# The first loads of an attention kernel: wq on ScalarE's queue, K and V in whole transfers from the first pack on

## The chip, the cores and the metric

The kernel runs on one core of one Trainium2 chip. The metric is the device time of one execution in microseconds (us). Before the change it is 732.18 us, the median of three runs (731.67 to 732.88). A profile of one execution was taken beside them. All times "at" some us are counted from the start of the profiled span.

## The reference

Two independent attention blocks, A and B, have the same shapes; their outputs stand side by side. For each block:

```python
B, Sq, D = 16, 64, 640          # x
H, Sk, Dh = 32, 512, 128        # k_cache, v_cache: [B, H, Sk, Dh]
q = (x @ wq).reshape(B, Sq, H, Dh).transpose(0, 2, 1, 3)      # wq: [640, 4096]
scores = einsum("bhqd,bhkd->bhqk", q, k_cache) * Dh ** -0.5
p = softmax(scores, axis=-1)
o = einsum("bhqk,bhkd->bhqd", p, v_cache)
out = o.transpose(0, 2, 1, 3).reshape(B, Sq, H * Dh) @ wo     # wo: [4096, 640]
```

Everything is bfloat16. K and V are read once each, 64 MiB per cache and block, so most of what the kernel moves is K and V.

## The kernel before, in words

**Packs, groups, phases.** A pack `n` is two batches by four heads: 1 MB (2 x 512 KB) of K and 1 MB of V. There are 128 packs. Four packs (`NJ`) form a group: the same two batches, 16 heads. Eight groups (`NBP`) form a phase of 32 packs: all batches with one half of a block's heads. Four phases (`ph`) cover A's two halves and then B's. A phase has its own half of wq (five transfers of 512 KB, `LDWQ`, one for each 128 rows of wq, in rows of 4 KB) and its own half of wo (four blocks of 640 KB, `LDWO`, in rows of 1280 bytes).

**The steps of a pack.** `XT`/`XE`/`XS`/`XC` transpose the group's x tile and put it where the projection reads it (`xT_ring`). `WP` (GpSimd, L656) reorders wq from `ws_sb` into `wqp_sb`; two copies per pack index make one pack's part, and the first of them waits for all five transfers. `QP` (TensorE, L688) is the q projection, `QE` scales q. `KT` (VectorE, L702) transposes K. `S` (L712) is the scores, `EX` (ScalarE) the exponential with its row sum, `RC` (VectorE) the reciprocals, `NM` (GpSimd) the multiplication by them. `TR` (TensorE, L774) and `TE` (VectorE) transpose the probabilities, `PV` (L867) multiplies them by V, `OE` evicts, `OP` (L887) multiplies by wo and adds up in PSUM. PV and what follows for a pack run about two packs behind its scores: TensorE does QP(n), PV(n-2), S(n), TR(n-1), OP(n-2) in turn. So the pipeline begins with packs -2 and -1, which have zeros in place of data. TensorE's instructions form a loop of four packs.

**The order of work.** `build_plan` makes all operations with a nominal time in packs (`AT`); each engine's order follows these times, and the waits are worked out from what the operations read and write. SP's list of loads is ordered by times of its own: in the kernel before, the first phase's five `LDWQ` come first (-50), then K of packs 0, 1, 2, the second group's x, V of pack 0, the first wo block, K 3, V 1, wo, K 4, V 2, wo, K 5, V 3, and so on. SP issues in this order and waits, where it has to, for a place in a ring: K has six places, V four. In V's ring, the places 2 and 3 are held at the start by the zeros of packs -2 and -1, so V of pack 2 waits for `TR(-1)`, V of pack 3 for `TR(0)`, V of pack 4 for `TR(1)`.

**Queues.** SP's transfers run on the DMA queue that the page calls q1, ScalarE's on q10. In the kernel before, ScalarE issues only the first x tile (`LDX`, L608). Each K and V ring place and each part of wq has a semaphore of its own; a first load from ScalarE has one of its own, too (`d_first`).

**Transfers.** The constant `KSPLIT` = 8 makes the first eight packs' K come in four transfers of 256 KB (L629) and their V in two of 512 KB (L646; the second half has another semaphore, and `TE` waits for the first, `PV` for the second). Later packs have two transfers of 512 KB for K (L631) and one of 1 MB for V (L641). The last two packs (`NARROW`) have their V in two parts in any case. The rows are the same in both forms: 8 KB for K, 4 KB for V.

The lines that decide this:

```python
apart = 0 <= n < cfg.KSPLIT or n >= N - cfg.NARROW
...
if i < 2 or n < cfg.KSPLIT:
    op = add("sp", "LDK", (n, i), n + AT["KT"] - 0.9, [], [("kn", n % cfg.NK)])
    loads.append((n - cfg.NV + AT["PV"] + 0.2 - cfg.KLEAD, 2, op))
```

Of the kernel before, what the change touches and what calls it, by code (L numbers as in the profile page):

```python
# [20 lines left out]
class Cfg:  # L21
# [8 lines left out]
    PERIOD = 4  # L30
    BASE = 32
    KLEAD = 2.5
    KSPLIT = 8
    NARROW = 2
    AFTER = 24
    AT = dict(XT=-2.585, XE=-2.383, XS=-1.65, XC=-0.788, QP=-0.428, QE=-0.224, KT=-0.672, S=0,
# [50 lines left out]
def build_plan(dims, cfg, general):  # L87
# [4 lines left out]
    NPH, NBP, NJ = dims["NPH"], dims["NBP"], dims["NJ"]  # L92
    PH = NBP * NJ
    N = NPH * PH
    AT = cfg.AT
    ops = []
    loads = []
    at = {}

    def add(eng, kind, idx, ts, reads=(), writes=()):  # L100
        op = Op(eng, kind, idx, ts, reads, writes)
        ops.append(op)
        at[(kind, idx)] = op
        return op

    def add_output(n):
        g, j = n // NJ, n % NJ
        final = n >= 0 and dims["FINAL"](g // NBP)
        apart = 0 <= n < cfg.KSPLIT or n >= N - cfg.NARROW
        for b in range(0 if apart else 1, 2):  # L110
# [61 lines left out]
    for ph in range(NPH):  # L172
        twp = [ph * PH + t for t in AT["WP1" if ph else "WP0"]]
        for kt in range(dims["KT"]):
            ready = (twp[-1] - PH if ph > 1 else AT["WP0"][-1]) + 0.5
            op = add("sp", "LDWQ", (ph, kt), twp[0] - 0.5 if ph else -20.0, [], [("ws", kt, j) for j in range(NJ)])
            loads.append((ready + 2.0 + 0.14 * PH * kt if ph > 1 else AT["PV"] + 0.15 if ph else -50.0, 1, op))
        for j in range(NJ):
            w = ph * NJ + j
            n0 = ph * PH + j  # L180
            for i in range(2):
                add("pool", "WP", (w, i), twp[2 * j + i], [("ws", kt, j) for kt in range(dims["KT"])], [("wqp", j, i)])
            if ph:
                loads.append((n0 - NJ + AT["LDWO"], 4, add("sp", "LDWO", w, n0 + AT["OP"] - 0.8 * NJ, [], [("wo", j)])))
            else:
                loads.append((n0 - 1.9, 4, add("sp", "LDWO", w, n0 + AT["OP"] - 0.8 * NJ, [], [("wo", j)])))
# [6 lines left out]
    for n in range(-2, N):  # L193
# [3 lines left out]
        g, j = n // NJ, n % NJ  # L197
        add("pe", "QP", n, n + AT["QP"], [("xT", g % cfg.NX), ("wqp", j, 0), ("wqp", j, 1)], [("SB", 1)])
        add("act", "QE", n, n + AT["QE"], [], [("SB", 1), ("qs", n % cfg.NQ)])
        for i in range(4):  # L200
            if i < 2 or n < cfg.KSPLIT:
                op = add("sp", "LDK", (n, i), n + AT["KT"] - 0.9, [], [("kn", n % cfg.NK)])
# [65 lines left out]
    def for_pe(d):  # L268
        if d.kind == "EX":
            return d.idx % 4 == 1 or d.idx % 4 == 0 and d.idx // 4 % NJ == 1  # L270
        if d.kind == "OE":
            return d.idx[1] == 0
        if d.kind == "LDV":
            return d.idx[1] == 1
        if d.kind == "NM":
            return d.idx % 4 == 3 and d.eng == "pool"
        if d.kind == "OS" and d.idx == N // NJ - 1:
            return False
        return d.kind in own
# [44 lines left out]
    counts = dict(base)  # L324

    def sem_key(op):
        if op.kind == "LDX" and op.eng == "act":
            return ("d_first",) + op.writes[0]
        if op.kind == "LDV":
            return ("d_v" if op.idx[1] else "d_vh", op.writes[0][1])  # L330
        if op.kind in LOADS:
            return ("d_" + op.kind[2:].lower(),) + op.writes[0][1:]
        if op.kind in ("ST", "STH"):
            return ("d_out",)
        return ("q_" + op.eng,) if for_pe(op) else ("s_" + op.kind.lower() + "_" + op.eng,)

    for eng in ENGINES:
        for op in progs[eng]:
            op.sem = sem_key(op)
            counts[op.sem] = op.count = counts.get(op.sem, 0) + 1  # L340
# [164 lines left out]
def mha_kernel(nc, blocks, out, cfg=None):  # L505
# [16 lines left out]
    def wide(n):  # L522
        return n < NPACK - cfg.NARROW

    plans = []
    for general in (False, True):
        dims = dict(NPH=NPH, NBP=NBP, NJ=NJ, KT=KT, FIRST=lambda ph: ph % NSUB == 0,
                    FINAL=lambda ph: ph % NSUB == NSUB - 1)
        plans.append(build_plan(dims, cfg, general))
    NK, NV, NKT, NX, NXN, NQ, NPN, NRS = (cfg.NK, cfg.NV, cfg.NKT, cfg.NX, cfg.NXN, cfg.NQ, cfg.NPN, cfg.NRS)  # L530

    with contextlib.ExitStack() as es:
# [42 lines left out]
        def pack_info(n):  # L575
            g, j = n // NJ, n % NJ
            ph = g // NBP
            return ph // NSUB, g % NBP, j, ph % NSUB * HPH + 4 * j
# [45 lines left out]
        def em_LDK(e, op):  # L624
            n, b, l = op.idx[0], op.idx[1] // 2, op.idx[1] % 2
            blk, bp, j, h = pack_info(n)
            src = blocks[blk][1][2 * bp:2 * bp + 2, h:h + 4].rearrange("b h (p l t) d -> l (h p) b (t d)", l=2, t=32)[l]
            if n < cfg.KSPLIT:
                ins = e.dma_start(kn_ring[2 * b + l::4, n % NK].rearrange("p a c -> p (a c)"), src[:, b])  # L629
# [4 lines left out]
        def em_LDV(e, op):  # L634
# [3 lines left out]
            blk, bp, j, h = pack_info(n)  # L638
            if wide(n) and n >= cfg.KSPLIT:
                src = blocks[blk][2][2 * bp:2 * bp + 2, h:h + 4].rearrange("b h (p t) d -> (h p) b (t d)", t=16)  # L640
# [430 lines left out]
```

## Time and profile before

| | |
|---|---|
| median of three runs | 732.18 us |
| the profiled execution | 732.12 us, of which the span is 730.4 us |
| TensorE busy (matmul) | 674.1 us, 92% |
| VectorE, ScalarE, GpSimd busy | 514.5, 533.3, 417.9 us |
| moved by DMA | 295.02 MB, mean 404 GB/s |
| first slice of 18.26 us | 337 GB/s |
| first wq: issued by SP | 0.93 to 3.32 us |
| first q projection on TensorE | 15.48 us |
| first scores | 20.08 us |
| SP waits for TensorE's transposes before a V load (L641) | 251.1 us in 105 waits |

The busy shares are means over the whole span; the slices of the page and the stretches of the trace tell when. In lines of the timeline the columns are start, duration, engine, line, operation, tiles and count, and in brackets the idle time before it with what ended it. SPq and ACTq are the issues of DMAs on SP's and ScalarE's queue. In the table of stretches each engine has its busy time and in brackets the number of instructions; the last three columns are the granted TensorE clock, the DMA engines' mean busy share and the GB/s that they moved.

### The profile page before, as it was taken

The page shows a single profiled execution, that of the slowest core. Times are in us where ns is not written, and L with a number is a line of the kernel's source. Part 1 is how long each engine was busy: PE and PEld are TensorE (multiplying, and loading weights), DVE is VectorE, ACT ScalarE, POOL GpSimd, SP SyncE. Part 2 cuts the span into 40 slices and gives each one's busy share as a digit, 9 for nine tenths or more (in the row PEclk, how much of TensorE's full clock was granted, in tenths as well). Part 3 has the DMA queues.
Part 4 walks back from the last instruction along what each step waited for, and adds up shares of the span by engine and source line. Part 5 has one row for each costly group of instructions (what it writes and reads, how often), then busy time and mean ns, then how long its engine had stood idle before and what let it go on. Part 6 is the DMA issues. An engine that isn't in the chain of part 4 may idle for free.

```text
span 730.4 us, 61195 instructions
## 1 busy us (share of the span) xinstructions
PE 674.1 (92%) x28502; PEld 530.3 (73%) x28502; DVE 514.5 (70%) x691; ACT 533.3 (73%) x1574; POOL 417.9 (57%) x596
## 2 busy tenths in 40 slices
PE   1679999999999999999997899999999799999998
PEld 1458778787777777777775677787777577787775
DVE  5447777777777766767765667677777567878775
ACT  1447878778787777777875677777778677878775
POOL 4436565666875455554884555465587446555552
PEclk9889999999999999999999999999999999999999
DMA  8999999999999999999999999999999999999993
GB/s 337 401 404 414 414 415 413 415 414 415 415 400 409 419 414 416 416 416 417 416 411 402 415 414 413 414 415 415 414 416 407 403 415 418 417 418 417 416 415 122
DMA packets 72336, 295.02 MB, mean 404 GB/s; under 512 B 7664, under 2 KB 20080, under 8 KB 55920
## 3 DMA queue, kind: packets, MB, share of 16 engines
q1 hardware_dynamic: 72160, 294.52, 100.0%
q8 instruction: 10, 0.16, 0.1%
q10 hardware_dynamic: 144, 0.16, 0.1%
q14 instruction: 22, 0.18, 0.1%
HBM read 292.03 MB, written 2.62 MB: 403 GB/s over the span
## 4 chain that ended last, share of the span: by engine, by line
PE 53%; DMA 32%; SPq 6%; DVE 3%; issue 3%; POOL 2%; ACT 1%; DVEq 0%; POOLq 0%
DMA xn_ring<-in_B_x_dram 14%; PE ps L867 12%; PE ps L887 11%; PE ps L688 11%; PE ps L712 10%; DMA kn_ring<-in_A_k_cache_dram 9%; PE ps L774 7%; DMA kn_ring<-in_B_k_cache_dram 5%; DMA wo_sb<-in_B_wo_dram 4%; SPq L631 4%; DVE kt_ring L702 2%; POOL pn_ring L762 2%; SPq L641 1%; DVE pT_sb L854 1%; SPq L615 1%
## 5 line engine op out<-in xcount | busy, mean ns | idle before, releaser
L762 POOL TENSOR_SCALAR pn_ring<-pn_ring,recip 128x512 bf16<-128x512 bf16 x508 | 343.4, 695 | 246.1 <-DVE recip L754 221.0
L702 DVE STREAM_TRANSPOSE kt_ring<-kn_ring 128x2048 f32<-128x2048 f32 x128 | 295.3, 2307 | 120.3 <-DMA kn_ring<-in_B_k_cache_dram 80.3
L741 ACT ACTIVATE pn_ring<-ps 128x512 bf16<-128x512 f32 x512 | 296.4, 592 | 5.7 <-PE ps L712 5.7
L854 DVE COPY pT_sb<-ps 128x1024 bf16<-128x1024 bf16 x256 | 168.4, 671 | 60.2 <-PE ps L774 60.2
L688 PE MATMUL ps<-xT_ring,wqp_sb 128*128 128x128 bf16 x2560 | 165.9, 220 | 11.6 <-POOL xT_ring L677 11.6
L867 PE MATMUL ps<-pT_sb,v_ring 32*128 32x64 bf16 x16448 | 162.2, 192 | 10.6 <-DVE pT_sb L854 4.6
L688 PEld LDWEIGHTS ps<-xT_ring,wqp_sb 128*128 128x128 bf16 x2560 | 157.5, 114 | 17.8 <-issue 11.8
L867 PEld LDWEIGHTS ps<-pT_sb,v_ring 32*128 32x128 bf16 x16448 | 147.0, 91 | 24.8 <-issue 12.5
L887 PE MATMUL ps<-wo_sb,oT_sb 128*128 128x320 bf16 x1024 | 163.5, 303 | 0.0
L875 ACT ACTIVATE oT_sb<-ps 128x256 bf16<-128x256 f32 x257 | 84.7, 381 | 95.1 <-PE ps L867 95.1
L712 PE MATMUL ps<-kt_ring,qs_ring 32*64 32x512 bf16 x4096 | 138.4, 380 | 4.8 <-issue 4.8
L694 ACT ACTIVATE qs_ring<-ps 128x512 bf16<-128x512 f32 x128 | 76.4, 597 | 76.5 <-PE ps L688 74.5
L774 PEld LDWEIGHTS ps<-ident,pn_ring 64*128 64x128 bf16 x4096 | 68.3, 95 | 77.0 <-ACT oT_sb L875 46.0
L887 PEld LDWEIGHTS ps<-wo_sb,oT_sb 128*128 128x128 bf16 x1024 | 90.4, 98 | 36.7
L741 ACT ACTIVATION_READ_ACCUMULATOR pn_ring<-ps 128x1 f32 x512 | 105.3, 206 | 0.0
L774 PE MATMUL ps<-ident,pn_ring 64*128 64x64 bf16 x4096 | 82.9, 191 | 22.8 <-POOL pn_ring L762 18.6
L712 PEld LDWEIGHTS ps<-kt_ring,qs_ring 32*64 32x64 bf16 x4096 | 53.4, 103 | 32.9 <-issue 5.5
L754 DVE RECIPROCAL recip<-rowsum 128x2 f32<-128x2 f32 x256 | 40.6, 158 | 27.6 <-ACT pn_ring L741 24.6
L879 ACT ACTIVATE ps<-zeros 128x256 f32<-128x256 bf16 x128 | 49.5, 387 | 4.1
L656 POOL COPY wqp_sb<-ws_sb 128x1280 bf16<-128x1280 bf16 x32 | 39.6, 1256 | 9.9 <-DMA ws_sb<-in_A_wq_dram 6.8
L668 ACT ACTIVATE xe_sb<-ps 128x640 bf16<-128x640 bf16 x32 | 22.9, 716 | 8.7 <-PE ps L662 8.6
L677 POOL COPY xT_ring<-xe_sb 128x640 bf16<-128x640 bf16 x16 | 11.5, 717 | 21.0 <-PE ps L774 21.0
(42 smaller groups left out, 103.5 us busy)
## 6 DMA issues: line engine op xcount, KB each, us to landing
kn_ring<-in_B_k_cache_dram SPq DMA_DIRECT2D x128, 512.0 KB, 16.1
v_ring<-in_B_v_cache_dram SPq DMA_DIRECT2D x62, 1024.0 KB, 16.5
kn_ring<-in_A_k_cache_dram SPq DMA_DIRECT2D x112, 512.0 KB, 11.4
v_ring<-in_A_v_cache_dram SPq DMA_DIRECT2D x56, 1024.0 KB, 14.8
kn_ring<-in_A_k_cache_dram SPq DMA_DIRECT2D x32, 256.0 KB, 8.6
v_ring<-in_A_v_cache_dram SPq DMA_DIRECT2D x16, 512.0 KB, 8.9
ws_sb<-in_A_wq_dram SPq DMA_DIRECT2D x10, 512.0 KB, 9.3
wo_sb<-in_A_wo_dram SPq DMA_DIRECT2D x8, 640.0 KB, 13.3
```

Of the source, the lines that this page charges most:

```text
L688: last = e.matmul(ps[:, 1, f * 128:(f + 1) * 128], w[:, kt, f, :], xT_ring[:, xs, kt, :], start=(kt == 0), stop=(kt == KT - 1))
L694: ins = e.activation(qs_ring[:, op.idx % NQ].rearrange("p f b q -> p (f b q)"), ps[:, 1, :], ACTF.Copy, scale=scale)
L702: ins = e.transpose(dst.rearrange("p c b (h l) -> p c h b l", h=8, l=2), src)
L712: last = e.matmul(ps[64 * b:64 * b + 64, i, :], qs_ring[rows, n % NQ, f, b, :], kt_ring[rows, n % NKT, :, f // 2, b, :, f % 2], start=(f = ...
L741: ins = e.activation(dst, src, ACTF.Exp, scale=1.0, accum_out=sum_of(h))
L762: ins = e.tensor_scalar(pn_view(h), pn_view(h), recip[:, h:h + 1], 1.0, ALU.mult, ALU.mult)
L774: last = e.transpose(pt_bank(b)[:, 64 * c:64 * c + 64], pn[rows, c, :], ident[rows, rows], tile_position=(64 * b, 0))
L854: ins = e.tensor_copy(pT_sb[:, b].rearrange("p t q -> p (t q)"), pt_bank(b))
L867: last = e.matmul(ps[:, 4 + i, 64 * b:64 * b + 64], v_ring[rows, n % NV, b, c, :], pT_sb[rows, b, c, :], start=(t == 0 and i < 2), stop=(t ...
L875: ins = e.activation(oT_sb[:, 2 * a:2 * a + 2, :], o_ps[:, 2 * a:2 * a + 2, :], ACTF.Copy)
L879: ins = e.activation(z_ps, zeros[:, :].unsqueeze(2).broadcast_to([128, 2, 128]), ACTF.Copy)
L887: last = e.matmul(out_ps[:, s, :], oT_sb[:, i, :], wo_sb[:, 4 * j + i, s * NH0:(s + 1) * NH0], start=(j == 0 and i == 0), stop=(j == NJ - ...
```

## The change

The first phase's five `LDWQ` go from SP to ScalarE, behind the first x load, each with a semaphore of its own; SP begins with K of pack 0 at once. `KSPLIT` becomes 0: K of every pack comes in two transfers of 512 KB, V of every pack but the last two in one of 1 MB. The later phases' wq stays on SP.

```diff
-    KSPLIT = 8
+    KSPLIT = 0
...
-            op = add("sp", "LDWQ", (ph, kt), twp[0] - 0.5 if ph else -20.0, [], [("ws", kt, j) for j in range(NJ)])
-            loads.append((ready + 2.0 + 0.14 * PH * kt if ph > 1 else AT["PV"] + 0.15 if ph else -50.0, 1, op))
+            op = add("sp" if ph else "act", "LDWQ", (ph, kt), twp[0] - 0.5 if ph else -20.0 + 0.1 * kt, [],
+                     [("ws", kt, j) for j in range(NJ)])
+            if ph:
+                loads.append((ready + 2.0 + 0.14 * PH * kt if ph > 1 else AT["PV"] + 0.15, 1, op))
...
-        if op.kind == "LDX" and op.eng == "act":
+        if op.kind in ("LDX", "LDWQ") and op.eng == "act":
             return ("d_first",) + op.writes[0]
```

## The prediction

> **What bounds the kernel now.** I read the page first (busy shares, the 40 slices), then the waits of SP's queue, then the first 60 us: the timeline, the table of stretches, the DMA queues in two short windows.
>
> ```profile
> DMA  8999999999999999999999999999999999999993
> GB/s 337 401 404 414 414 415 413 415 414 415 415 400 409 419 414 416 416 416 417 416 411 402 415 414 413 414 415 415 414 416 407 403 415 418 417 418 417 416 415 122
> ```
>
> The slices show one resource that is full from the second slice to the last but one: the DMA engines, at some 415 GB/s. 295 MB at that rate are 711 us of the 730.4 us span. TensorE is at 92% but is never the one that lets DMA go idle. So the end moves only if DMA bytes move earlier or later, or if DMA runs dry. In the first slice DMA has 337 GB/s; that is where the change acts.
>
> ```profile
> 0.00:8.00 8.00, 0.69 (x5) 0.45 (x5) 5.33 (x3) 1.99 (x2) 1.45 (x8) 1.00 0.69 234
> 8.00:10.00 2.00, 0.00 (x0) 0.00 (x0) 2.00 (x1) 0.00 (x0) 0.00 (x0) 1.00 1.02 404
> 10.00:12.00 2.00, 0.00 (x0) 0.00 (x0) 0.10 (x1) 0.00 (x0) 0.00 (x0) 1.00 1.04 432
> 8.00:16.00 8.00, 0.52 (x6) 0.55 (x7) 3.27 (x2) 0.00 (x0) 3.78 (x4) 1.00 1.02 420
> 16.00:34.85 18.85, 11.80 (x430) 8.76 (x429) 8.11 (x9) 6.59 (x19) 10.97 (x11) 0.87 1.03 401
> 34.85:53.81 18.96, 14.52 (x446) 10.57 (x447) 8.10 (x11) 8.26 (x25) 6.09 (x9) 0.76 1.03 403
> 60.00:200.00 140.00, 140.00 (x6124) 111.08 (x6122) 109.50 (x145) 113.18 (x336) 89.32 (x129) 1.00 1.02 415
> ```
>
> These stretches (the last two columns are the DMA share and GB/s) give how many bytes had moved by any time: 1.87 MB at 8 us, 5.23 MB at 16 us, 12.79 MB at 34.85 us. From 8 us on DMA is full. In 60 to 200 us PE is busy throughout too: both run at the same pace there.
>
> ```profile
> 0.93 2.39 SPq L615 DMA_DIRECT2D ws_sb<-in_A_wq_dram  x5
> 3.37 8.96 SPq L629 DMA_DIRECT2D kn_ring<-in_A_k_cache_dram  x12
> 12.22 2.45 POOL L656 COPY wqp_sb<-ws_sb 128x1280 bf16<-128x1280 bf16 x2 [6.80 <-DMA ws_sb<-in_A_wq_dram]
> 14.83 2.31 DVE L702 STREAM_TRANSPOSE kt_ring<-kn_ring 128x2048 f32<-128x2048 f32 x1 [4.74 <-DMA kn_ring<-in_A_k_cache_dram]
> 15.48 2.29 PE L688 MATMUL ps<-xT_ring,wqp_sb 128*128 128x128 bf16 x20 [11.58 <-POOL xT_ring L677]
> 18.38 1.78 PE L867 MATMUL ps<-pT_sb,v_ring 32*128 32x64 bf16 x128 [0.60 <-DVE pT_sb L852]
> 20.08 1.07 PE L712 MATMUL ps<-kt_ring,qs_ring 32*64 32x512 bf16 x32
> 34.85 0.82 SPq L646 DMA_DIRECT2D v_ring<-in_A_v_cache_dram  x2
> ```
>
> The timeline gives the order of the start: wq lands at 12.22 us (POOL's wait for it ends), K of pack 0 at 14.83 us, the first q projection starts at 15.48, the first PV (of empty pack -2) at 18.38, the first scores at 20.08. The last line is the first place where SP has to wait for PE: V of pack 3 needs the transposes of pack 0, and SP had issued everything ahead of it by 29.95 us.
>
> **The cushion.** Ahead of that V, SP had issued wq 2.62 MB, two x tiles 0.33, K of six packs 6.29, V of three packs 3.15, three wo blocks 1.97: 14.36 MB. Moved were 12.79, so 1.57 MB or 3.8 us of work lay in the queue. The same sum at the V of pack 5 (53.81 us): 14.36 + 7.63 issued in between, less 12.79 + 403 GB/s x 18.96 us = 7.64, again 1.56 MB. As V and K then follow PE pack by pack, those 3.8 us are all that stands between a late PE and an idle DMA for some 30 packs.
>
> **The edits.** (a) Whole transfers. K of packs 0 to 7 goes from 32 issues to 16, V from 16 to 8. In the trace's packet records a K row (8 KB) takes 309 ns and a V row (4 KB) 159 ns whatever the size of the transfer, and each transfer's semaphore write 9 ns: 24 x 9 ns = 0.2 us gained. SP's own issue time (0.59 us for a K issue of 256 KB in its line's group, and 1.18 us for two of 512 KB later) is halved, but DMA was full from 8 us on, so it is hidden by the backlog. [...]
>
> (b) ScalarE issues the five wq transfers behind its x load. Each issue took 0.39 to 0.48 us on SP, some 2.2 us in all, ahead of the table load (1.28 us) and the copy of x (3.94 us today, then about 4.9). SP's second x load waits for that copy, with V and wo behind it, about 1 us at 4.5 us, while over 4 MB are queued. The copy's result is needed behind wq only. Cost nothing.
>
> (c) The order of the bytes. Today wq is ahead of all K on one queue. Then the queues share the engines from the first byte, and wq, which the first projection waits for, comes later. How two queues share, the trace shows once, where the x load (ScalarE's q10) meets wq (q1):
>
> ```profile
> q10 hardware_dynamic: 88, 0.11, 51.8%
> ...
> q1 hardware_dynamic: 19, 0.08, 48.3%
> q10 hardware_dynamic: 56, 0.05, 38.9%
> ```
>
> The first line is 1.5 to 2.36 us, the others 2.36 to 2.75 us. The packet records have q10's 16 semaphore writes at 2.36 to 2.72 us, and each of q1's first rows starts within about 10 ns of one: an engine finishes its share of one transfer (8 rows and the semaphore) and only then turns to the other queue. A share of wq and of a K transfer are both 32 KB, so I take turns of equal bytes: wq ends when 5 x 0.52 MB of wq, 5 x 0.52 of K and the x tile, 5.40 MB, have moved. By the table that is 16.4 us. Landing lags this average: today wq with x is 2.79 MB, moved at 10.3 us, and landed 1.9 us later; K of pack 0, 3.83 MB, likewise 2.1 us. With 0 to 2 us of lag wq lands at 16.4 to 18.4; I take 17.9, since most of the lag was there in two rows. If the slow first 8 us were gone it would be 2.4 + 5.40 MB / 418 GB/s = 15.3 us.
>
> From landing to the first scores: two copies and xT, 3.26 us (12.22 to 15.48), the projection 2.29, the PV 1.7 up to the scores: 7.3 us. (Today 7.86: the PV also waited 0.6 us for memsets behind K's transpose, which will be long done.) So the first scores come at 25.2 instead of 20.08, X = 5.1 us (2.5 to 5.6). PE's next packs run through pauses of 1.64, 4.81 and 3.98 us that the page calls issue, with six fetches on the instruction queue between 17 and 60 us; they come after the first PV, so I move them along unchanged.
>
> (d) The wait that this adds. V of pack 3 comes X later, at about 40 us, with wo, K of pack 6 and the next wq behind it on SP. The 14.36 MB are moved by 38.7 us. DMA is dry, and it starts again only when a new issue delivers: 1.03 us from the x load's issue to its first packet, 1.44 for wq's, which q10 held up. So the cushion can shrink to 1.0 to 2.4 us unpunished; I take 1.6, near the second row and a little for engines that run dry first. Loss: X - (3.8 - 1.6) = 5.1 - 2.2 = 2.9 us, between 0 and 4.2. What DMA gained before it ran dry, the 0.2 us of (a), is lost with it, since PE's progress then sets the issues. Nothing later gives it back: DMA is full to the end.
>
> [...]
>
> **Sum.** The profiled execution took 732.12 us (span 730.4 and 1.7 around it), 0.06 below the median of 732.18. 732.12 + 2.9 = 735.0 us.
>
> **Rivals.** (1) ScalarE's queue is emptied first. The x load shows an engine finishing q10 before q1; with only one transfer in q10 it cannot show whether the engine would have gone on to a second. Then wq lands at about 12.2 and K at 14.8 as today, and the time is 732.0. A lag of zero with a fast start (15.3 us, X = 2.5) ends close by, at 0.3 us over. (2) Turns in which K gets more than wq, for instance row by row: wq has 40 rows per engine; beside them go 24 K rows, 8 of x and 8 of V, 3.83 MB. 6.61 MB are moved at 19.4 us, landing 20.9, scores 28.2, X = 8.2, loss 6.0: 738.1. Against it: no q1 row between q10's rows on an engine above; for it: a K transfer's share is 4 rows and a semaphore write where the x load's was 8 and one, so two could go in one turn, which would land wq later still. [...] (3) Faster: the first 8 us moved 1.87 MB where 415 GB/s from 2.4 us on would have moved 2.33 MB. If two queues fill the engines where one did not, that 0.46 MB is 1.1 us, with (a) 1.3: 730.8. It decides only if wq still lands by 13.7, as X plus the gain has to stay under 2.2; so it needs a fast start and most of the turns for wq. The slow rows and the uneven landing speak for a start with something to win, equal shares against.
>
> **Numbers.** The forecast has 0.58, rival 1 with its neighbour 0.18, rival 2 0.12, rival 3 0.12. A measurement of this kernel tells apart about 0.2%, 1.5 us (its three runs lie within 1.2). Of the forecast's case 0.08 falls within that. Slower 0.50 + 0.12 = 0.62, same 0.18 + 0.08 = 0.26, faster 0.12. The range takes in the forecast's 732.1 to 736.3, rival 1 less half the spread of the runs (0.6 us), and rival 2 up to its time: 731.4 to 738.1; the forecast's own side alone is 733.6 to 736.3.
>
> **What would show it.** POOL's wait for wq ends near 17.9 us instead of 12.22; K's transpose is no longer waited for; first scores near 25; SP's wait for V of pack 3 ends near 40 with a dip of DMA under 0.9 at 38 to 42 us; K's time to landing in 55 to 65 us falls from 8.3 to about 6 us. Wrong would be: wq landing by 14 us; PE's pauses becoming shorter as DMA is lighter, which would take X back; or no dip at 40 us with X over 4, which would mean that the cushion was larger than 3.8 us.

## The result: 7.2 us slower

The changed kernel takes 739.47 us in the median (738.77 to 739.95), the kernel before, run beside it, 732.26 us (731.67 to 732.88). The ratio is 1.010, with a 95% interval of 1.0087 to 1.0113. I had said 735.0 us, with a range up to 738.1: the sign was right, the loss was two and a half times as large as I said, and the time lies above the range. The profiled execution has a span of 737.9 us, 7.5 longer than before's.

The slices of the page first, the changed kernel's:

```profile
DMA  9989999999999999999999999999999999999993
GB/s 334 385 300 396 404 416 414 413 415 415 417 405 405 416 416 417 416 417 414 418 412 403 411 413 414 414 414 417 412 416 408 402 415 416 418 416 417 416 413 111
```

The loss can be seen in the second and above all the third slice (36.9 to 55.3 us): 300 GB/s where before had 404. From the sixth slice on the two rows are nearly the same, so what was lost in the first 70 us is not given back. The first slice has 334 against 337: over these 18 us two queues moved no more. What they had ahead in the first 8 us (262 GB/s against 234) was given back in the next 8 (385 against 420).

The timeline of the changed kernel, its start and then the issue of pack 3's V:

```profile
0.93 3.89 SPq L633 DMA_DIRECT2D kn_ring<-in_A_k_cache_dram  x6
1.21 3.12 ACTq L617 DMA_DIRECT2D ws_sb<-in_A_wq_dram  x5
13.84 2.31 DVE L704 STREAM_TRANSPOSE kt_ring<-kn_ring 128x2048 f32<-128x2048 f32 x1 [0.49 <-DMA kn_ring<-in_A_k_cache_dram]
20.48 2.45 POOL L658 COPY wqp_sb<-ws_sb 128x1280 bf16<-128x1280 bf16 x2 [13.35 <-DMA ws_sb<-in_A_wq_dram]
23.74 2.30 PE L690 MATMUL ps<-xT_ring,wqp_sb 128*128 128x128 bf16 x20 [19.80 <-POOL xT_ring L679]
27.79 1.93 PE L714 MATMUL ps<-kt_ring,qs_ring 32*64 32x512 bf16 x32
...
42.29 0.37 SPq L643 DMA_DIRECT2D v_ring<-in_A_v_cache_dram  x1
```

GpSimd's wait for wq ends at 20.48 us, not at 12.22 (before) nor at 17.9 (forecast). VectorE's 13.84 is already its second K transpose: K is early now and waits for q. The first scores come at 27.79 us, 7.7 us later than before. V of pack 3 is issued at 42.29 us where before issued it at 34.85. The waits of SP's queue say the same in one line, here from 0 to 70 us:

```profile
SPq L643 <- PE ps L776: 32.4, 5, 9.2
```

SP stood 32.4 us in five waits for TensorE's transposes, the longest 9.2 us. What that did to DMA is seen in the table of stretches (the last three columns are the granted TensorE clock, the DMA share and GB/s):

```profile
8.00:16.00 8.00, 0.00 (x0) 0.00 (x0) 7.40 (x5) 0.00 (x0) 0.00 (x0) 1.00 1.00 385
36.00:38.00 2.00, 0.00 (x0) 0.00 (x0) 0.00 (x0) 0.00 (x0) 0.47 (x1) 0.63 1.07 396
38.00:40.00 2.00, 0.20 (x8) 0.19 (x15) 0.00 (x0) 0.00 (x0) 0.00 (x0) 0.50 0.76 306
40.00:42.00 2.00, 2.00 (x49) 1.01 (x35) 0.00 (x0) 0.67 (x3) 0.00 (x0) 0.50 0.15 53
42.00:44.00 2.00, 2.00 (x21) 1.29 (x16) 1.36 (x3) 1.75 (x7) 0.25 (x1) 0.66 0.27 33
44.00:46.00 2.00, 2.00 (x98) 1.88 (x95) 1.96 (x3) 1.28 (x2) 2.00 (x4) 1.00 0.94 365
```

The queue is dry before SP gets to issue. The 16 engines run out one after the other from 39.0 to 41.25 us, V is issued at 42.29, its first row starts at 43.33, and the rate is back from 44.4 on.

The same can be told in one number, DMA's lag: how much earlier the kernel before had moved the same bytes. It is 0.1 us at 30 us, 1.2 at 40, 4.8 at 44, 5.5 at 50, 6.7 at 75 us, and then stays there (6.8 at 700 us). I use it for every run below, beside the lateness of TensorE: when a pack's scores start, against before.

### The profile page after: what moved, and what is told of

Read it like the earlier page. It is cut to its first block, busy times and chain, and to the rows that moved or that the text cites. A ratio compares the mean times of both kernels' runs of the same rounds, so it can differ in the third digit from the quotient of the medians.

```text
span 737.9 us, 61163 instructions
## 1 busy us (share of the span) xinstructions
PE 674.4 (91%) x28502; PEld 530.0 (72%) x28502; DVE 514.2 (70%) x691; ACT 533.3 (72%) x1574; POOL 417.8 (57%) x596
## 4 chain that ended last, share of the span: by engine, by line
PE 57%; DMA 28%; SPq 5%; DVE 3%; issue 3%; POOL 2%; ACT 1%; ACTq 0%; DVEq 0%; POOLq 0%
PE ps L869 14%; PE ps L889 12%; PE ps L690 12%; PE ps L714 11%; DMA kn_ring<-in_A_k_cache_dram 7%; DMA kn_ring<-in_B_k_cache_dram 7%; PE ps L776 7%; DMA xn_ring<-in_B_x_dram 7%; DMA wo_sb<-in_B_wo_dram 4%; SPq L633 3%; DMA ws_sb<-in_A_wq_dram 2%; DVE kt_ring L704 2%; POOL pn_ring L764 1%; DVE pT_sb L856 1%; SPq L643 1%
```

## How the two queues share the engines

The DMA queues of the changed kernel from 8 to 16 us (packets, MB, share of the 16 engines):

```profile
q1 hardware_dynamic: 296, 1.97, 63.4%
q10 hardware_dynamic: 298, 1.09, 36.5%
```

SP's q1 (mostly K, rows of 8 KB) and ScalarE's q10 (wq, rows of 4 KB) had the same number of packets and nearly twice the bytes for q1. A packet is a row or a semaphore write: q1's 296 are 241 rows and 55 semaphore writes, q10's 298 are 266 and 32. The packet records do not name the engine, but where one record starts within a few ns of the end of another, the two follow each other on one engine. One engine's order reads, between 8 and 16 us:

```
, w K w K w K w K ; , w K w K w K w K w , w K w K w K ;
```

(K and w are rows, the comma is a semaphore write of q1, the semicolon one of q10.) In these 8 us an engine took one packet from each queue in turn, and a semaphore write counted as a turn: of the 317 places where it is clear which record follows which, the queue changes at all 317. At the start it was not so. From 2.4 to 5.5 us the queue changes at 26 of 75 such places: several rows of one queue followed each other on an engine, as in the x load that I had read in the kernel before. Why the turns were longer there, the traces do not show.

So the turns of my second rival, row by row, are what happened from 8 us on. It had wq landing at 20.9, scores at 28.2 and X, TensorE's lateness, at 8.2; measured are 20.48, 27.79 and 7.7.

## The experiments

Two theories stood from here on. By the first, the lateness of TensorE's start is all of the loss: it eats the queue's cushion, and whatever is left shows in DMA's lag. Its rivals put the loss, or part of it, on the transfers' size, on the order or rate of the early bytes, or on a second queue as such. Each experiment ran in five rounds beside the kernel before, whose medians in the three groups were 732.67, 732.06 and 732.01 us.

**One part of the change each.** e1 is the kernel before with `KSPLIT = 0` (whole transfers, wq still ahead on SP). e2 is the changed kernel with `KSPLIT = 8` (wq on ScalarE, small transfers).

> The kernel before with KSPLIT = 0: whole transfers from the first pack on, wq still first on SP's queue. Theory R (the time is lost only by wq's place: it takes turns with K, row by row, and lands late): 732.0 us, no change within 0.2%, wq landing near 12.2 us. Theory W (whole transfers hurt, by coarser landing of K and V in the first packs): more than 734 us.

> The changed kernel with KSPLIT = 8 again: wq on ScalarE's queue, K of the first packs in 256 KB transfers. Theory R (turns by rows): K's rows are still 8 KB, so wq lands near 20 us and the time is 739 to 740 us. Theory T (turns by transfers): a turn of K is half as large, wq lands by 17 us, and the time is 735 to 737 us.

e1 took 732.91 us, ratio 1.0001 (0.9991 to 1.0011). e2 took 738.87 us, ratio 1.0081 (1.0063 to 1.0099). GpSimd's wait for wq in the timelines of e1 and then e2:

```profile
12.36 2.44 POOL L656 COPY wqp_sb<-ws_sb 128x1280 bf16<-128x1280 bf16 x2 [6.92 <-DMA ws_sb<-in_A_wq_dram]
```

```profile
19.74 2.44 POOL L658 COPY wqp_sb<-ws_sb 128x1280 bf16<-128x1280 bf16 x2 [12.12 <-DMA ws_sb<-in_A_wq_dram]
```

Whole transfers alone neither cost nor bring anything. The move of wq is most of the loss: e2 lost 6 of the changed kernel's 7 us, and wq landed far from the 17 us of theory T. But it landed 0.74 us earlier than in the changed kernel, and DMA's lag was 5.85 us, not 6.7. The queues of e2 from 8 to 16 us show a reason:

```profile
q1 hardware_dynamic: 346, 1.91, 60.7%
q10 hardware_dynamic: 345, 1.23, 40.8%
```

The packets are equal in number again. With K in transfers of 256 KB an engine has a semaphore write behind every second K row instead of every fourth, so 113 of q1's packets are semaphore writes, where the changed kernel has 55. Each takes a turn, and wq moves 1.23 MB in these 8 us instead of 1.09.

**The size of the rows.** e3 is the changed kernel with K of the first three packs in 4 KB rows, in four transfers a pack. If the turn is one row, wq and K then get equal bytes.

```diff
-            if n < cfg.KSPLIT:
-                ins = e.dma_start(kn_ring[2 * b + l::4, n % NK].rearrange("p a c -> p (a c)"), src[:, b])
+            if n < cfg.K4:                                   # K4 = 3
+                ins = e.dma_start(kn_ring[l::2, n % NK, b], src[:, :, b * 2048:(b + 1) * 2048])
```

> The changed kernel with K of packs 0 to 2 in rows of 4 KB (four transfers of 64 rows, same bytes). Theory R (turns by rows): beside wq's 40 rows per engine go 40 K rows of half the size, so 5.4 MB instead of 6.6 have to move: wq lands 2 to 3 us earlier than the 20.5 us of the changed kernel, at about 18, and the time is 736.5 to 737.5 us. Theory B (the queues share by bytes or time, and wq is slow for another reason): wq lands at 20.5 us as before and the time stays at 739.5 us.

```profile
18.28 2.44 POOL L659 COPY wqp_sb<-ws_sb 128x1280 bf16<-128x1280 bf16 x2 [10.45 <-DMA ws_sb<-in_A_wq_dram]
```

```profile
q10 hardware_dynamic: 466, 1.68, 51.6%
q1 hardware_dynamic: 486, 1.60, 50.0%
```

wq landed at 18.28 us, 2.2 us earlier than in the changed kernel. The length of K's rows is not all of that, since these K transfers are also 256 KB, as in e2; against e2's 19.74 us the shorter rows brought 1.5 us. The second block has the queues from 8 to 16 us: with rows of one length the bytes are now as equal as the packets. This is the test of the turns, and row by row passed it. TensorE was 5.0 us late and DMA's lag 4.4 us. The time missed the 736.5 to 737.5 us that I expected: 738.91 us (736.5 to 739.52), ratio 1.0077 (1.0059 to 1.0095), while the profiled execution, the fastest of the six, took 736.5. What the other executions lost besides, the one trace cannot show.

**The late start alone.** e4, e5 and e11 are the kernel before, with its DMA order untouched: GpSimd makes 4, 2 and 7 more copies of 1.2 us each ahead of the first wq copy, into a buffer that is not in use yet. So only TensorE's start is late.

```diff
+            for d in range(7 if op.idx == (0, 0) else 0):    # 4 in e4, 2 in e5
+                ins = e.tensor_copy(acc[:, 7 - d].bitcast(BF16).rearrange(...), part)
+                first = first or ins
             ins = e.tensor_copy(dst[:, :, :, jj], part)
```

> The kernel before with four more copies of the size of the first wq copy on GpSimd ahead of that copy (they write an accumulator that is not in use yet): the order of all DMA bytes is untouched, only TensorE's first projection comes later, by 4 x 1.25 = 5.0 us; the first scores by about 4.4 (0.6 us of slack). Theory C1 (the prediction's cushion: 2.2 us of lateness cost nothing): 734.4 us. Theory C2 (the queue's 3.8 us of work is no slack, the end follows TensorE's start but for some 0.5 us): 736 us. Theory C3 (DMA's order, not TensorE's start, makes the loss): 732.2 us.

> The kernel before with two more copies on GpSimd instead of four ahead of the first wq copy. With four, the first scores came 4.0 us later, SP's V of pack 5 went out 2.6 us later and DMA fell behind by 1.65 us. Here the first scores should come 1.7 us later and V of pack 5 by 1 us at most. Theory C4 (the queue needs about 3 us of work at each V issue to keep every engine busy, so about 1 us of lateness is free): 732.7 us, no change within 0.2%. Theory C2 (no lateness is free): 734.0 us or more.

> The kernel before with seven more copies on GpSimd ahead of the first wq copy: order and size of all transfers are those of before, TensorE's first scores come some 7.4 us later, about as late as in the changed kernel (7.7). Theory L (the late start of TensorE is the whole loss, by making SP wait and DMA run dry near 40 us): 738 to 740 us, with a DMA gap like that of the changed kernel. Theory M (the mixed queues cost DMA something of their own): at least 2 us less than the changed kernel, under 737.5 us.

The timeline of e11, and its stretches:

```profile
12.26 8.43 POOL L659 COPY acc<-ws_sb 128x1280 bf16<-128x1280 bf16 x7 [6.76 <-DMA ws_sb<-in_A_wq_dram]
23.88 2.29 PE L693 MATMUL ps<-xT_ring,wqp_sb 128*128 128x128 bf16 x20 [19.91 <-POOL xT_ring L682]
27.93 1.61 PE L717 MATMUL ps<-kt_ring,qs_ring 32*64 32x512 bf16 x32
...
42.43 0.81 SPq L646 DMA_DIRECT2D v_ring<-in_A_v_cache_dram  x2
```

```profile
38.00:40.00 2.00, 0.06 (x8) 0.06 (x15) 0.00 (x0) 0.00 (x0) 0.00 (x0) 0.50 0.58 234
40.00:42.00 2.00, 2.00 (x44) 1.00 (x45) 0.00 (x0) 0.52 (x2) 0.00 (x0) 0.50 0.04 12
42.00:44.00 2.00, 2.00 (x23) 1.22 (x18) 1.36 (x3) 1.90 (x8) 0.03 (x1) 0.50 0.25 25
```

With wq landing at 12.26 us, in one queue, the first projection starts 0.14 us later than in the changed kernel; V of pack 3 is issued 0.14 us later and the hole in DMA is much the same. e11 took 739.02 us, as theory L expected, ratio 1.0100 (1.0085 to 1.0114): as much as the changed kernel lost at first, without the second queue. The changed kernel run once more beside it (e12) took 740.14 us, ratio 1.0110 (1.0095 to 1.0124). That is 1.1 us more than e11; e12's packs 3 to 36 were 0.9 us later than e11's and its lag 1.0 us larger, so this part goes with TensorE's lateness too. The intervals overlap, and a cost of the second queue under 1 us is not ruled out.

> The changed kernel once more, beside the other two on one chip: 739 to 740 us.

The smaller doses tell how far the cushion goes:

| run | scores of pack 0 late | packs 3 to 36 late | DMA's lag at 100 us | V of pack 3 issued | work queued then | ratio (interval) |
|---|---|---|---|---|---|---|
| e5 | 1.7 us | 1.1 us | 0.35 us | 35.77 | 2.8 us | 1.0028 (1.0018 to 1.0038) |
| e4 | 4.0 | 2.6 | 1.7 | 38.05 | 0.9 | 1.0042 (1.0027 to 1.0057) |
| after | 7.7 | 7.8 | 6.6 | 42.29 | 0 | 1.0100 (1.0087 to 1.0113) |
| e11 | 7.9 | 7.2 | 6.2 | 42.43 | 0 | 1.0100 (1.0085 to 1.0114) |
| e12 | 7.6 | 8.2 | 7.2 | 42.23 | 0 | 1.0110 (1.0095 to 1.0124) |

The queued work is counted from the packets; the kernel before has 3.9 us by this count. In all five, DMA's lag is the lateness of packs 3 to 36 less 0.8 to 1.2 us. So, by DMA's lag, some 1.0 us of the queued work could be spent, where I had 2.2. e4 lost with work still queued: 0.9 us of it when V came, and DMA dropped to 260 GB/s and a busy share of 0.74 from 38 to 40 us. That fits engines that ran dry one by one, as in the changed kernel (39.0 to 41.25 us). e5 lost nothing at this V, with 2.8 us queued, and 0.5 us between 60 and 75 us, after V issues at 60 and 65 us with 2.7 and 2.9 us queued. After the hole, the work queued at the V issues of the changed kernel and of e11 was back at 3.2 us by 77 us and 3.7 by 118.

The times of e4 (735.77 us) and e5 (733.92 us) do not show the free 1.0 us. They rose by 1.4 and 1.5 us more than DMA's lag, and lie at the 736 and near the 734.0 us of theory C2, by which no lateness is free; C1's 734.4 and C4's 732.7 did not come. But e5's 1.9 us are also more than the 1.1 to 1.7 us by which TensorE was late, so C2 does not explain them either. That part is open (below).

**A deeper queue.** e8 and e9 let K run one pack further ahead (`KLEAD` 2.5 to 3.5), e8 in the changed kernel, e9 in the kernel before.

> The changed kernel with KLEAD = 3.5 instead of 2.5: in SP's order K goes out one pack further ahead of V, so 1.05 MB or 2.5 us more lies in the queue at each wait for a place in V's ring. Theory Q (the loss is DMA running dry while SP waits for PE, lateness less spare work): 2.5 us come back, 736.5 to 737.5 us. Theory P (the end follows TensorE's late start whatever lies in the queue): 739.5 us, as the changed kernel.

> The kernel before with KLEAD = 3.5. DMA does not run dry there, so theory Q expects 732.3 to 732.8 us, no change within 0.2%; a gain of more than 0.2% would say that DMA has idle time in the kernel before that the stretches do not show.

e8 took 740.29 us, ratio 1.0117 (1.0099 to 1.0135), not theory Q's 736.5 to 737.5. Eight K transfers were issued ahead of SP's x load, where the changed kernel has six, and wq landed at 22.18 us, later still:

```profile
22.18 2.44 POOL L658 COPY wqp_sb<-ws_sb 128x1280 bf16<-128x1280 bf16 x2 [15.02 <-DMA ws_sb<-in_A_wq_dram]
```

TensorE was 9.3 us late in packs 3 to 36 and DMA's lag 6.1: the lag fell short of the lateness by 3.2 us instead of 1. The extra 1.05 MB of K, 2.5 us at 415 GB/s, can be spent nearly in full (2.2 us). But the last V comes later in this order: from the last K or V row to the end it is 16.8 us instead of 15.2. e9 shows that price by itself, 16.7 instead of 15.6 us, at 733.23 us (732.3 to 732.8 expected), ratio 1.0016 (1.0007 to 1.0025). The expected gain of e8 was used up by the later wq and by the end.

**K held back.** e10 is the changed kernel with SP's second x load put ahead of K. That load waits for ScalarE's copy of the first x tile, so K is issued from 6.33 us on.

```diff
-  loads.append((txt - 3.7, 0, add("sp", "LDX", g, ...
+  loads.append((-50.0 if g == 1 else txt - 3.7, 0, add("sp", "LDX", g, ...
```

> The changed kernel with SP's x load of the second group ahead of K of pack 0: SP waits for ScalarE's copy of x, so K goes out from about 6.4 us instead of 0.93, and wq has the engines alone until then. Theory R (turns by rows): some 1.45 MB of wq move alone, the rest takes turns; wq lands at 16 to 17 us instead of 20.5, PE stays 3.5 to 4.5 us late from pack 3 on (7.8 in the changed kernel), and the time is 735 to 736.5 us. If wq's place among the bytes did not matter it would stay at 739.5 us.

```profile
6.33 4.66 SPq L633 DMA_DIRECT2D kn_ring<-in_A_k_cache_dram  x6
13.45 2.45 POOL L658 COPY wqp_sb<-ws_sb 128x1280 bf16<-128x1280 bf16 x2 [6.81 <-DMA ws_sb<-in_A_wq_dram]
```

wq landed at 13.45 us, earlier than the 16 to 17 us that I expected: K's first row started at 10.51 us behind those of x, when 608 of wq's 640 rows had started. Turns from the first moment do not explain this. The x load, issued at 5.88 us, had its first row at 9.62 us, 3.7 us later instead of 1.0; why q1 waited so long behind q10 is not shown. The first scores were 0.7 us late and the time 733.36 us (731.66 to 737.33), ratio 1.0025 (1.0011 to 1.0038). Two queues, whole transfers, and most of the loss gone: what matters is what K's rows do to wq.

**An earlier start.** e6 is the kernel before with the first phase's wq in two parts: the quarter that the first pack of each group needs (rows of 1 KB), then K of pack 0, then the rest.

```diff
-            loads.append((... else -50.0, 1, op))
+                    loads.append((-4.55 if part else -50.0, 1, op))    # for part in range(2): 1 of 4 columns, then 3
```

> The kernel before with the first phase's wq in two parts on SP: first the 512 columns of pack 0's heads (five transfers of 128 KB, rows of 1 KB), then K of pack 0, then the other three quarters. The first scores should come some 4 us earlier, at about 16 us. Theory D (before the change DMA is full from 8 us on and sets the end): 732.0 to 732.7 us, no gain within 0.2%. Theory E (the end follows TensorE's start in both directions): 728 to 729 us.

```profile
8.99 2.30 PE L694 MATMUL ps<-xT_ring,wqp_sb 128*128 128x128 bf16 x20 [4.72 <-POOL xT_ring L683]
```

```profile
GB/s 293 402 403 416 413 415 414 415 413 417 416 399 409 418 416 415 417 416 418 416 411 402 415 414 414 413 414 416 413 416 407 405 415 416 416 416 417 417 411 105
```

The first projection started at 8.99 us and the scores 3.5 us earlier than in the kernel before. It brought nothing: 734.43 us, ratio 1.0030 (1.0018 to 1.0042). The first slice of DMA fell from 337 to 293 GB/s, and DMA was 1.9 us behind from 12 us to the end. Without these 1.9 us the time would be 732.5 us, as theory D has it; theory E's 728 to 729 did not come. An earlier TensorE gained nothing here, where DMA is the bound, and the lost bytes cost in full.

No version tried beats the kernel before. The nearest is e1, which equals it.

## Why the prediction was right or wrong

- **(a) Whole transfers: right.** 0.2 us gained and hidden was the forecast; e1 measured +0.01% with a half interval of 0.1%. Together with wq on ScalarE they made that loss larger, by about 0.9 us of lag (the changed kernel against e2), where fewer semaphore writes (55 against 113 from 8 to 16 us) left more turns to K's rows (241 against 233).
- **(b) ScalarE's issues cost nothing: right.** They ended at 4.33 us. The copy of x came at 5.66 us, somewhat later than the 4.9 forecast, and nothing hung on it: GpSimd had been waiting for wq alone for 13.35 us when it landed.
- **(c) The order of the bytes: wrong in size, and the step that failed is "turns of equal bytes".** I took an engine's whole share of a transfer as its turn, from one place at the very start of a trace. From 8 us on the turn was one packet, K's rows are twice as long as wq's, and wq got 1.09 of 3.06 MB, a little over a third of the bytes, instead of half. wq landed at 20.48, not 17.9, and X was 7.7, not 5.1: 2.6 us of the miss. I had the row-by-row case as a rival at 0.12 and argued against it from that same place. The 7.3 us from landing to the first scores were right (27.79 - 20.48 = 7.31).
- **TensorE's pauses move along: right in sum.** The changed kernel has them at 35 to 40 and 48 to 53 us (lines below). They were not unchanged one by one: 0.50, 4.70 and 4.90 us against 1.64, 4.81 and 3.98 before. In sum they are 10.1 against 10.4 us, and none of the lateness came back: 7.7 us at pack 0, 7.8 in packs 3 to 36.

```profile
39.80 1.49 PE L714 MATMUL ps<-kt_ring,qs_ring 32*64 32x512 bf16 x19 [4.70 <-issue]
52.82 0.77 PE L776 MATMUL ps<-ident,pn_ring 64*128 64x64 bf16 x22 [4.90 <-issue]
```

- **(d) The cushion: right in kind, its term mis-sized.** The dip came (38 to 42 us in the forecast, 38 to 44 measured) and nothing gave it back. But I let the cushion shrink to 1.6 us unpunished; DMA's lag grew after V issues that found 0.9 us queued in e4, 2.7 and 2.9 in e5, and not after one that found 2.8 in e5. My 1.03 to 1.44 us for a restart held for the first row (1.03 us from issue to row, again), but I allowed next to nothing for engines that run dry over 2.2 us, nor for the first 1.1 us after, at 66 GB/s from 43 to 44 us. That is another 1.2 us.
- **The sum.** 5.1 - 2.2 = 2.9 was forecast. With the measured terms it is 7.7 - 1.0 = 6.7, which is DMA's lag from 75 us on. The 1.0 is itself read from these lags, so that this sum agrees is no test of it; the test of the cause is e11. The medians differ by 7.2, so 0.5 us is left.
- **The range** stopped at rival 2's 738.1, which was made with the same spendable 2.2 us. Its X came out within 0.5 us. With a cushion of 1.0 it would have been 739.3, and the result is 739.5: the range left out that both terms could be wrong together. Rival 1 (ScalarE's queue emptied first) and rival 3 (a faster start) are ruled out by the rows in turn and by 334 GB/s in the first slice.
- **What would show it.** Transfers now land sooner, as forecast, though the forecast was for K, whose landing this view does not give: the one V issued in 55 to 65 us took 6.4 us, where before's V (in halves) took 8.4 and its K 8.3.

**What stays open.** Between DMA's lag at 100 us and the loss in time there is a difference that the experiments do not settle: 0.3 to 0.9 us in the changed kernel (both times), e2, e6, e10 and e11, 1.4 to 1.8 us in e3, e4 and e5, and hardly any in e1. The lag is that of the profiled execution alone, and in e3 and e4 this was the fastest of the six. In e5 it was not, and there the trace shows a part: TensorE's lateness grows from 1.1 us at pack 36 to 1.5 at pack 44 and 2.0 at pack 80. Nor is it known why the executions of e3 are up to 3 us apart, those of e10 up to 5.7, and why the turns of the two queues begin late.

## What to carry to other kernels

Here the move of a load to another engine's queue did not only take its issues (2.39 us) from SP: it put wq beside the K that it had been ahead of. From 8 to 16 us the two full queues took turns packet by packet, and the one with rows of 8 KB moved 1.97 MB, the one with rows of 4 KB 1.09. So keep what the first step waits for ahead of the rest on one queue, or hold the other queue back until it has nearly landed. Where DMA is the bound, add up the work that lies queued when the issuing engine next has to wait, and do not take all of it as free to spend: here DMA lost after V issues that found 0.9, 2.7 and 2.9 us of work queued (e4 and e5).

## What the runs showed of the hardware that was not expected

- In the changed kernel two full queues alternated single packets, rows or semaphore writes: 296 and 298 from 8 to 16 us, with rows of 8 and 4 KB. With more semaphore writes on K's side (113 against 55) wq landed 0.7 us earlier (e2), with K rows of 4 KB another 1.5 us earlier (e3). From 2.4 to 5.5 us the queue changed at 26 of 75 places. In e10 608 of wq's 640 rows had started before K's first.
- In the changed kernel the 16 engines did not run dry at once: their last bytes ended 2.2 us apart (39.0 to 41.25 us), and after the issue into empty queues at 42.29 us it took 1.0 us to the first row and another 1.1 us to the full rate.
